# Moving the remaining key, query and value loads of a fused attention and MLP kernel into its MLP stages, with a fourth output buffer

## The chip, the cores and the metric

The kernel runs on one core of a Trainium2 chip. The metric is the device time of one execution in microseconds (us), taken as the median of several runs. The core's engines are named as the profile names them: PE (matrix multiply) and PEld (its weight loads, which overlap the multiplies), DVE (vector engine), ACT (activation engine), POOL (GpSimd) and SP (which here only issues DMAs). A DMA issued by POOL goes through queue 0 of the profile ("software_dynamic"), one issued by SP or ACT through queue 1 ("hardware_dynamic"). Each engine works through its own list of instructions in order and waits on semaphores for the others.

## The reference

Forgetting attention for 8 batches of 8 heads, 576 positions, head size 64, and then an MLP with a tanh-gelu over the 4608 rows that come out of it. Cut to what is computed:

```python
scores = scale * q @ k.T                     # per batch and head
log_f  = log(clip(f, 1e-4, 1.0)); cum = cumsum(log_f)
scores = where(causal, -1e9, scores + cum[:, None] - cum[None, :])
attn   = softmax(scores) @ v                 # [8, 8, 576, 64]
x      = attn.transpose(0, 2, 1, 3).reshape(4608, 512)
h      = x @ w_in                            # [4608, 2048]
out    = gelu_tanh(h) @ w_out                # [4608, 512] f32
```

All inputs are float32 in HBM; the weights and q, k are cast to bf16 on the way in, by the DMA.

## The kernel before

**Units of work.** Attention is done by quads: a quad is four heads of one batch, so there are 16 quads, two to a batch (quad 6 and 7 belong to batch 3, quad 8 and 9 to batch 4, and so on). The MLP is done by chunks of 512 rows, nine of them, 0 to 8. The rows of chunk c need the batches up to c, so the program runs the MLP of chunk c beside the attention of the quads 2c+2 to 2c+4.

**Stages.** For the chunks 1 to 7 the order alternates between two stages. In the MLP stage of chunk c the first matrix product and its gelu run (`P` and `R` in the tables, lines 363 and 412; PE writes `ps_h`, `ps_ab`, `ps_cd`). Its multiplies have 128 columns of weights each. In the attention stage that follows, the scores, the softmax and the value products of two quads (`S`, `D`, `V`; PE tiles `ps_s`, `po`) are woven between pieces of the second matrix product of the same chunk (`f`, line 497; PE tile `ps_w`), and there nearly every multiply is cut into four of 32 columns that run side by side, so this stage has many more PE instructions for each microsecond.

**What sets the order.** The order of all work is written out by hand, in tables of words that are played in order (`run`, line 709, for `FRONT`, which holds the start and chunks 0 and 1; `play`, line 747, for `TABLES[2]` to `TABLES[8]`). A word's place fixes where its instructions stand in the list of each engine that it uses. In the tables `q3` and `q4` stand for quads 2c+3 and 2c+4, `q5` and `q6` for 2c+5 and 2c+6; a word for a quad above 15 does nothing. The words that matter here:

- `LK.i` and `LQ.i` (line 190): POOL issues the load of quad i's keys or queries, 288 KB each, into `k_c[i % 2]` or `q_c[i % 2]`. There are two buffers of each, so a load has to wait until quad i-2 has been transposed out of its buffer.
- `TK.i` and `TQ.i` (lines 205 and 208): DVE transposes them into `kT` and `qT`.
- `LV.b.half` in `FRONT` and `LV` in the tables (lines 165, 665, 743): SP issues the five loads of the values of half a batch or of a whole one into `v_nat[b % 2]`; in `TABLES[c]` it is batch c+2. `LX.b.half` is the same issued by POOL. `@LK.6` after a word makes its first DMA wait for that load to land.
- `M.i.r` (line 271): POOL masks round r of a quad's scores with `affine_select`, after ACT's exponential (line 269). `VW.i` (line 211): POOL multiplies the values by the decay weights; `vw.i` does so on DVE.
- `S.i.r` (line 243): PE scores and ACT's exponential of round r of a quad. `CL.i`: a small DVE copy. `K` and `T`: DVE sums for the first product's blocks.
- `O.512`: what is left of the second product of the chunk before.

**Where the loads stand before.** In `TABLES[2]` all of `LK.q5 LQ.q5 LK.q6 LQ.q6 LV` lie in the MLP stage. In `TABLES[3]` and `TABLES[4]` the loads of `q5` lie in the MLP stage and those of `q6` (quad 12 and quad 14) in the attention stage, behind `M.q3.2`. In `TABLES[5]` `q6` would be quad 16, which does not exist. In `FRONT`, `LQ.8` lies inside the attention stage of chunk 1, and `LK.7`, `LK.8` and the five loads of `LX.3.1` (quad 7's values) lie at its end, on POOL.

**Buffers.** The results of the second product go through `o_st`, tiles of 128x512 float32 in a ring of three (`ostage_pool`, line 119), from which SP stores them. The gate input f is read into `f_sb` (line 149), used in the first microseconds only. `g1`, `g2`, `g4` (trace name `gsum`) hold sums of gelu outputs and are first written in the MLP stage of chunk 1.

Of the kernel before, what the change touches and what calls it, by code (L numbers as in the profile page):

```python
# [16 lines left out]
def kernel(  # L17
# [770 lines left out]
```

## Time and profile before

| | us |
|---|---|
| median of 3 runs | 330.29 (330.05 to 330.64) |
| the profiled execution | 330.31 |
| its span, from first to last instruction | 328.6 |
| PE busy in it | 315.0 |
| DVE busy | 231.8 |
| ACT busy | 202.2 |
| POOL busy | 111.6 |

The granted clock of PE was 0.999 of full speed over the span. The profile counts an engine as busy while one of its instructions runs; matrix multiplies overlap each other, so a busy PE need not be at its peak. Where an engine stood idle, the profile names what ended the wait. "issue" means that it found nothing that the engine waited for: no semaphore of another engine and no DMA of the program. Beside the queues of the program's own DMAs, the profile shows queues of kind "instruction": packets that bring code. Queue shares are shares of the time of 16 DMA engines.

### The profile page before, as it was taken

How to read it: one execution, taken by the hardware profiler on the slowest of the kernel's cores; microseconds unless marked ns; L12 is line 12 of the kernel's file. 1: busy time of each engine (PE TensorE's matmuls, PEld its weight loads, DVE VectorE, ACT ScalarE, POOL GpSimd, SP SyncE). 2: the span in 40 equal slices, each digit the busy share in tenths (PEclk: the TensorE clock that was granted, in tenths of full speed). 3: DMA queues.
4: the chain of work that ended last, by engine and by line, in shares of the span. 5: the costliest groups of instructions: out<-in, count | busy, mean ns of one | idle time of the engine just before them, and what ended most of it. 6: DMA issues, size and time to landing. Idle time of an engine off the chain costs nothing.

```text
span 328.6 us, 12085 instructions
## 1 busy us (share of the span) xinstructions
PE 315.0 (96%) x5443; PEld 211.7 (64%) x5463; DVE 231.8 (71%) x363; ACT 202.2 (62%) x239; POOL 111.6 (34%) x155
## 2 busy tenths in 40 slices
PE   3999999999999999999979999999999999999995
PEld 1357844545775467656756577657775787687684
DVE  4686139894876865778856997798778658785772
ACT  4685677775766676668637785678666841721630
POOL 8986563510415318102740248022720150000000
PEclk9999999999999999999999999999999999999999
DMA  7999999861125990284158615581020103012002
GB/s 127 206 210 215 164 229 205 161 159 38 36 40 106 240 213 9 68 177 74 36 108 182 100 38 104 146 128 50 33 69 2 34 6 98 0 34 96 3 33 96
DMA packets 44324, 33.43 MB, mean 102 GB/s; under 512 B 27488, under 2 KB 37856, under 8 KB 44272
## 3 DMA queue, kind: packets, MB, share of 16 engines
q0 software_dynamic: 8848, 16.58, 28.9%
q1 hardware_dynamic: 35280, 16.01, 18.9%
q8 instruction: 42, 0.69, 0.9%
q14 instruction: 10, 0.08, 0.1%
q10 hardware_dynamic: 144, 0.07, 0.1%
HBM read 36.85 MB, written 9.44 MB: 141 GB/s over the span
## 4 chain that ended last, share of the span: by engine, by line
PE 93%; POOL 2%; issue 2%; ACT 1%; DVE 1%; DMA 1%; POOLq 0%; DVEq 0%; ACTq 0%
PE ps_w L510 29%; PE ps_h L374 25%; PE ps_s L261 10%; PE po L329 10%; PE ps_h L464 4%; PE pso L580 4%; PE ps_cd L422 4%; PE ps_ab L422 3%; PE po_m L315 1%; PE idle_ps L240 1%; ACT pt L269 1%; POOL v_nat L169 1%; DMA out_dram<-o_st 1%; PE ps_o L329 0%; DVE pt L304 0%
## 5 line engine op out<-in xcount | busy, mean ns | idle before, releaser
L269 ACT ACTIVATE pt<-ps_s 128x1024 bf16<-128x1024 f32 (+2 forms) x100 | 93.7, 988 | 41.4 <-PE ps_s L261 36.9
L374 PE MATMUL ps_h<-xT,w_in_sb 128*128 128x512 bf16 x368 | 85.5, 379 | 0.8
L381 ACT ACTIVATE gT<-ps_h 128x1024 bf16<-128x1024 f32 x48 | 49.0, 1021 | 42.9 <-PE ps_h L374 42.8
L275 POOL TENSOR_SCALAR_AFFINE_SELECT pt<-pt 128x512 bf16<-128x512 bf16 (+3 forms) x65 | 39.1, 611 | 99.4 <-ACT pt L269 98.4
L374 PEld LDWEIGHTS <-w_in_sb 128*128 128x128 bf16 x384 | 37.4, 98 | 40.9 <-issue 0.4
L510 PEld LDWEIGHTS <-gT 128*32 128x32 bf16 (+1 forms) x1247 | 51.3, 97 | 6.3 <-issue 1.7
L510 PE MATMUL ps_w<-w_out_sb,gT 128*32 128x256 bf16 (+1 forms) x1050 | 47.2, 273 | 0.0
L510 PEld LDWEIGHTS <-gsum 128*32 128x32 bf16 (+1 forms) x1256 | 39.3, 97 | 3.2 <-issue 1.9
L261 PE MATMUL ps_s<-qT,kT 32*128 32x64 bf16 (+5 forms) x896 | 37.0, 265 | 0.5 <-issue 0.4
L198 DVE STREAM_TRANSPOSE kT<-k_c 128x576 f32<-128x576 f32 x16 | 20.0, 1248 | 17.6 <-DMA k_c<-in_k_dram 17.6
L510 PE MATMUL ps_w<-usum,gsum 128*32 128x256 bf16 (+1 forms) x832 | 30.8, 273 | 0.0
L535 DVE TENSOR_TENSOR o_st<-ps_w,snap 128x512 f32<-128x512 f32 x31 | 21.3, 690 | 13.0 <-PE ps_w L510 12.1
L215 POOL TENSOR_TENSOR vw<-v_nat,wT 128x1280 bf16<-128x1280 f32 (+1 forms) x13 | 30.4, 2337 | 0.1
L360 DVE TENSOR_TENSOR xT<-po,rb 128x576 bf16<-128x576 f32 x26 | 19.6, 754 | 12.8 <-PE po L329 12.5
L261 PEld LDWEIGHTS <-kT 32*128 32x128 bf16 x896 | 17.0, 93 | 17.6 <-issue 12.5
L192 POOL DMA_DIRECT2D k_c<-in_k_dram x16 | 9.2, 576 | 44.0 <-DVE kT L198 38.8
L329 PE MATMUL po<-pt,vw 128*32 128x64 bf16 (+4 forms) x624 | 22.9, 279 | 0.0
L329 PEld LDWEIGHTS <-vw 128*32 128x32 bf16 x672 | 14.5, 96 | 10.7 <-issue 4.0
L198 DVE STREAM_TRANSPOSE qT<-q_c 128x576 f32<-128x576 f32 x16 | 19.9, 1244 | 1.1 <-DMA q_c<-in_q_dram 1.1
L489 DVE TENSOR_TENSOR gsum<-gT 128x1024 bf16<-128x1024 bf16 x16 | 11.0, 685 | 11.0 <-ACT gT L381 11.0
L510 PE MATMUL ps_w<-w_out_sb,gsum 128*32 128x256 bf16 (+1 forms) x400 | 15.6, 273 | 1.7 <-issue 1.7
L169 POOL DMA_DIRECT2D v_nat<-in_v_dram x20 | 15.3, 775 | 4.6 <-DMA w_out_sb<-in_moe_w_out_dram 4.6
(100 smaller groups left out, 398.0 us busy)
## 6 DMA issues: line engine op xcount, KB each, us to landing
out_dram<-o_st SPq DMA_DIRECT2D x35, 256.0 KB, 2.2
k_c<-in_k_dram POOLq DMA_DIRECT2D x16, 288.0 KB, 4.9
q_c<-in_q_dram POOLq DMA_DIRECT2D x16, 288.0 KB, 5.5
v_nat<-in_v_dram SPq DMA_DIRECT2D x16, 256.0 KB, 4.7
w_in_sb<-in_moe_w_in_dram POOLq DMA_DIRECT2D x4, 512.0 KB, 9.3
w_out_sb<-in_moe_w_out_dram POOLq DMA_DIRECT2D x4, 512.0 KB, 8.4
v_nat<-in_v_dram SPq DMA_DIRECT2D x16, 128.0 KB, 3.0
v_nat<-in_v_dram POOLq DMA_DIRECT2D x13, 128.0 KB, 7.2
```

The source lines that it names most:

```text
L198: nc.vector.transpose(out=dst.rearrange("p s c -> p (s c)").bitcast(FP32) .rearrange("p (t a) -> p a t", a=S // 32), in_=src.rearrange("p ...
L215: eng.tensor_mul(vw[i % 2][:, t0:t1], vb[:, t0:t1, h0:h0 + 4, :], wT[:, i, t0:t1, :].unsqueeze(3).to_broadcast([128, t1 - t0, 4, D]))
L261: nc.tensor.matmul(tiles[h // 2][:, h % 2, c0:c0 + nq], key_columns(i, key, h, c), qq[32 * h:32 * h + 32, q0:q0 + nq, c], start=(c == 0 an ...
L269: nc.scalar.activation(p[:, 2 * g:2 * g + 2, off:off + n], t[:, :, 0:n], AF.Exp, scale=scale)
L275: nc.gpsimd.affine_select(out=x, in_=x, compare_op=ALU.is_ge, fill=0.0, base=0, pattern=pattern, channel_multiplier=-1)
L329: nc.tensor.matmul(po[r0:r0 + w.shape[-1], 448 + q0:448 + q0 + nq], w, p[:, h, col:col + nq], start=(key in (0, "low")), stop=(key in ("lo ...
L360: nc.vector.tensor_mul(xT[:, 2 * u + x, S * b + s0:S * b + s1], po, rbs[i, part])
L374: nc.tensor.matmul(ph[:, j, :], w_in_sb[:, dt, 128 * ft:128 * ft + 128], xT[:, dt, CH * c:CH * (c + 1)], start=(dt == 0), stop=(dt == N_DT ...
L381: nc.scalar.activation(gT[:, 2 * pr:2 * pr + 2, :], ph, AF.Gelu_apprx_tanh)
L422: nc.tensor.matmul(ps[:, j], w[:, dt, 128 * j:128 * j + 128], x[:, dt], start=(first and j == 0 and dt == 0), stop=(dt == 1), skip_group_c ...
L510: nc.tensor.matmul(ps[c0:c0 + width, n, cols[0]:cols[1]], x[:, j, 128 * n + c0:128 * n + c0 + width], w[:, j, cols[0]:cols[1]], start=(fir ...
L535: nc.vector.tensor_add(st, ps, kept[name])
```

## The change

The loads change places, on three edits of tables, and two buffers change.

1. `FRONT`: `LV.3.1` (SP) follows `LV.3.0@LQ.7`; `LK.7 LQ.8 LK.8` follow `M.4.0`; all in the MLP stage of chunk 1. `LQ.8` inside the attention stage and `LK.7 LK.8` and `LX.3.1@LK.6` at its end are gone. So the five value loads pass from POOL's queue to SP's.
2. `TABLES[3]` and `TABLES[4]` lose `LK.q6 LQ.q6` from the attention stage; `TABLES[4]` and `TABLES[5]` begin with `Y O.512 LK.q4 LQ.q4`, which are the same quads, 12 and 14, one chunk later. `TABLES[5]` also loses `LK.q6 LQ.q6`, which did nothing.
3. The ring of `o_st` has four tiles; `f_sb` is no tile of its own any more but the first 576 float32 of the first 64 partitions of `g2`.

No instruction of PE, DVE or ACT is added, removed or moved in its engine's order; POOL's list loses five DMA issues and SP's gains five.

```diff
@@ FRONT
-        v.3.0 f.0.3 H.4.2.0 CL.4 I.1.0 m.4.1 U.0 LV.2.1@LQ.5 I.1.4 TQ.6 m.4.2.3 I.1.1 I.1.5 U.1 LV.3.0@LQ.7 m.4.2.2 TK.6 G.0 M.4.0 I.1.2 I.1.3 U.3
-        I.1.6 I.1.7 G.1.1.2 U.2 X F.1.16 S.5.0 f.1.26 S.5.1 D.4 M.5.0 f.1.16 S.5.2 V.4.0 m.5.2.3 f.1.10 VW.5 V.4.1 CL.5 m.5.2.2 LQ.8 S.6.0 f.1.10 M.5.1
-        D.5 f.1.7 S.6.1 V.5.1 f.1.12 V.5.0 vw.6 S.6.2 m.6.1 M.6.2.2 m.6.0 m.6.2.3 LK.7 LK.8 CL.6 LX.3.1@LK.6
...
+        LQ.7 VW.4 H.4.0.0 V.3.1 v.3.0 f.0.3 H.4.2.0 CL.4 I.1.0 m.4.1 U.0 LV.2.1@LQ.5 I.1.4 TQ.6 m.4.2.3 I.1.1 I.1.5 U.1 LV.3.0@LQ.7 LV.3.1 m.4.2.2
+        TK.6 G.0 M.4.0 LK.7 LQ.8 LK.8 I.1.2 I.1.3 U.3 I.1.6 I.1.7 G.1.1.2 U.2 X F.1.16 S.5.0 f.1.26 S.5.1 D.4 M.5.0 f.1.16 S.5.2 V.4.0 m.5.2.3
+        f.1.10 VW.5 V.4.1 CL.5 m.5.2.2 S.6.0 f.1.10 M.5.1 D.5 f.1.7 S.6.1 V.5.1 f.1.12 V.5.0 vw.6 S.6.2 m.6.1 M.6.2.2 m.6.0 m.6.2.3 CL.6
@@ TABLES[3]
-        TK.q4 TQ.q4 M.q3.1 VW.q3 f.18 S.q3.2 V.q2.1 M.q3.2 LK.q6 LQ.q6 CL.q3 f.16 S.q4.0 VW.q4 D.q3 M.q4.0 f.18 S.q4.1 V.q3.0 M.q4.1 f.9 V.q3.1 f.7 T
+        TK.q4 TQ.q4 M.q3.1 VW.q3 f.18 S.q3.2 V.q2.1 M.q3.2 CL.q3 f.16 S.q4.0 VW.q4 D.q3 M.q4.0 f.18 S.q4.1 V.q3.0 M.q4.1 f.9 V.q3.1 f.7 T CL.q4
@@ TABLES[4]
-        Y O.512 P.0.1 R.1 P.4.1 R.1 R.1 TK.q3 TQ.q3 LK.q5 LQ.q5 M.q2.2 LV P.2 G.0 P.3 P.6 P.7 G.1.1.2 X F.10 S.q3.0 D.q2 M.q3.0 f.22 S.q3.1 V.q2.0
-        TK.q4 TQ.q4 M.q3.1 VW.q3 f.18 S.q3.2 V.q2.1 K.3.0 K.3.1 M.q3.2 LK.q6 LQ.q6 CL.q3 f.16 S.q4.0 VW.q4 D.q3 M.q4.0 f.18 S.q4.1 V.q3.0 K.3.2 M.q4.1
+        Y O.512 LK.q4 LQ.q4 P.0.1 R.1 P.4.1 R.1 R.1 TK.q3 TQ.q3 LK.q5 LQ.q5 M.q2.2 LV P.2 G.0 P.3 P.6 P.7 G.1.1.2 X F.10 S.q3.0 D.q2 M.q3.0 f.22
+        S.q3.1 V.q2.0 TK.q4 TQ.q4 M.q3.1 VW.q3 f.18 S.q3.2 V.q2.1 K.3.0 K.3.1 M.q3.2 CL.q3 f.16 S.q4.0 VW.q4 D.q3 M.q4.0 f.18 S.q4.1 V.q3.0 K.3.2
...
@@ TABLES[5]
-        Y O.512 P.0.1 R.1 P.4.1 R.1 R.1 TK.q3 TQ.q3 LK.q5 LQ.q5 M.q2.2 LV P.2 G.0 P.3 P.6 P.7 G.1.1.2 X F.10 S.q3.0 D.q2 M.q3.0 f.22 S.q3.1 V.q2.0
+        Y O.512 LK.q4 LQ.q4 P.0.1 R.1 P.4.1 R.1 R.1 TK.q3 TQ.q3 LK.q5 LQ.q5 M.q2.2 LV P.2 G.0 P.3 P.6 P.7 G.1.1.2 X F.10 S.q3.0 D.q2 M.q3.0 f.22
...
-    ostage_pool = ctx.enter_context(tc.tile_pool(name="ostage", bufs=3))
+    ostage_pool = ctx.enter_context(tc.tile_pool(name="ostage", bufs=4))
...
-    f_sb = singles.tile([BH, S], FP32, name="f_sb")
+    f_sb = g2.rearrange("p t n -> p (t n)").bitcast(FP32)[0:BH, 0:S]
```

More of the change, by code (lines that the diff above doesn't have):

```diff
@@ L74 @@
         TQ.0 B.2.256 TK.1 SB TR LP.2@LQ.0 B.2.128 CW S.0.0 B.5.384 B.1.256 Z TQ.1 vw.0.0 S.0.2 WI.0 LQ.2 M.0.0 B.3.384 H.1.0.1 LP.3 B.1.256 vw.1.0
-        WI.1@LU.4 W H.1.1.1 WI.3 B.2.256 WI.2 H.1.0.0 M.1.0.1 D.0.0 M.1.0.0 H.0.1.1 V.0.0.0 H.0.1.0 B.2.256 M.0.1 H.1.1.0 V.0.1.0 D.1.0 H.0.3.0 B.2.128
-        V.1.0.0 LX.1.1 H.0.3.1 V.1.1.0 m.0.3.2 H.1.3.0 m.0.3.4 B.1.256 VW.1.1 H.1.3.1 B.4.128 vw.0.1 D.0.1 M.1.3 S.1.2 M.1.1 LK.2 V.0.1.1 V.0.0.1 WO.0
-        J.0.1 D.1.1 J.0.0 WO.1@LV.1.1 V.1.1.1 V.1.0.1 J.0.3 WO.2@WI.1 VW.3 J.1.0 WO.3 LK.3 LQ.3 J.1.1 TQ.2 J.1.3 LQ.4 LX.1.0@WO.2 TK.2 J.0.2 J.1.2 X
@@ L82 @@
-        D.5 f.1.7 S.6.1 V.5.1 f.1.12 V.5.0 vw.6 S.6.2 m.6.1 M.6.2.2 m.6.0 m.6.2.3 LK.7 LK.8 CL.6 LX.3.1@LK.6
+        WI.1@LU.4 W H.1.1.1 WI.3 B.2.256 WI.2 H.1.0.0 M.1.0.1 D.0.0 M.1.0.0 H.0.1.1 V.0.0.0 H.0.1.0 B.2.256 M.0.1 H.1.1.0 V.0.1.0 D.1.0 H.0.3.0
+        B.2.128 V.1.0.0 LX.1.1 H.0.3.1 V.1.1.0 m.0.3.2 H.1.3.0 m.0.3.4 B.1.256 VW.1.1 H.1.3.1 B.4.128 vw.0.1 D.0.1 M.1.3 S.1.2 M.1.1 LK.2 V.0.1.1
+        V.0.0.1 WO.0 J.0.1 D.1.1 J.0.0 WO.1@LV.1.1 V.1.1.1 V.1.0.1 J.0.3 WO.2@WI.1 VW.3 J.1.0 WO.3 LK.3 LQ.3 J.1.1 TQ.2 J.1.3 LQ.4 LX.1.0@WO.2 TK.2
@@ new lines @@
+        J.0.2 J.1.2 X LK.4 F.0.6 TK.3 B.3.256 S.2.0 LK.5 F.0.9 S.2.2 F.0.10 S.2.1 TQ.3 TQ.4 F.0.10 LV.2.0@LK.5 m.2.1 vw.2 TK.4 S.3.0 f.0.1 M.2.2
+        CL.2 LQ.5 M.2.0 D.2 f.0.6 S.3.1 m.3.0 F.0.6 V.2.0 S.3.2 TK.5 LK.6 M.3.2 f.0.7 V.2.1 CL.3 S.4.1 m.3.1 LQ.6 F.0.6 TQ.5 H.4.2.1 D.3 H.4.0.1
+        LQ.7 VW.4 H.4.0.0 V.3.1 v.3.0 f.0.3 H.4.2.0 CL.4 I.1.0 m.4.1 U.0 LV.2.1@LQ.5 I.1.4 TQ.6 m.4.2.3 I.1.1 I.1.5 U.1 LV.3.0@LQ.7 LV.3.1 m.4.2.2
+        TK.6 G.0 M.4.0 LK.7 LQ.8 LK.8 I.1.2 I.1.3 U.3 I.1.6 I.1.7 G.1.1.2 U.2 X F.1.16 S.5.0 f.1.26 S.5.1 D.4 M.5.0 f.1.16 S.5.2 V.4.0 m.5.2.3
```

10 lines of the change are left out of this document (4 added, 6 removed).

## The prediction

> **What bounds the kernel now.** I read the page first: engines, then the DMA queues.
>
> ```profile
> span 328.6 us, 12085 instructions
> PE 315.0 (96%) x5443; PEld 211.7 (64%) x5463; DVE 231.8 (71%) x363; ACT 202.2 (62%) x239; POOL 111.6 (34%) x155
> ...
> q8 instruction: 42, 0.69, 0.9%
> ```
>
> PE is busy all but 13.6 us of the span, and none of the moved work is PE's, so a gain can only come from the places where PE waits. The third line is code: 42 packets of 0.69/42 MB, 16.4 KB. PE has 5443 + 5463 = 10,906 instructions, 260 for each of these packets. No other engine has a tenth as many, so queue 8 brings PE's program, a block of about 260 instructions at a time.
>
> Second, the windows view with one row per stage, from chunk 1's attention to chunk 6's MLP (columns: stretch; its length; busy time and instructions of PE, PEld, DVE, ACT, POOL; granted clock; DMA share; GB/s).
>
> ```profile
> 81.39:102.18 20.79, 20.74 (x614) 15.96 (x613) 16.25 (x25) 14.96 (x17) 5.26 (x5) 1.00 0.22 56
> 102.18:115.72 13.54, 13.49 (x63) 6.19 (x64) 8.98 (x12) 8.63 (x10) 7.57 (x12) 1.00 0.96 181
> 115.72:137.92 22.20, 21.70 (x641) 16.28 (x639) 14.99 (x27) 14.73 (x17) 9.44 (x10) 1.00 0.43 98
> 137.92:151.07 13.15, 13.10 (x75) 7.37 (x76) 10.49 (x13) 8.97 (x12) 2.36 (x4) 1.00 0.77 141
> 151.07:173.97 22.90, 21.14 (x639) 15.99 (x639) 16.67 (x29) 14.71 (x17) 10.35 (x12) 1.00 0.34 74
> 173.97:187.12 13.15, 13.09 (x75) 7.39 (x76) 10.44 (x13) 9.01 (x12) 2.36 (x4) 1.00 0.78 141
> 187.12:208.05 20.93, 20.88 (x640) 15.92 (x639) 17.54 (x29) 14.71 (x17) 10.62 (x12) 1.00 0.35 78
> 221.20:242.14 20.94, 20.89 (x640) 15.95 (x640) 16.01 (x26) 14.71 (x17) 9.22 (x10) 1.00 0.18 50
> 242.14:255.28 13.14, 13.09 (x75) 7.40 (x76) 9.81 (x14) 8.99 (x12) 1.23 (x2) 1.00 0.07 24
> ```
>
> The four attention stages of chunks 2 to 5 (rows 3, 5, 7, 8) hold the same PE work, yet take 22.20, 22.90, 20.93 and 20.94 us. So chunk 2 loses 1.27 us and chunk 3 loses 1.97 against chunk 4. The MLP stages lose nothing to transfers: 13.15 us with a DMA share of 0.77, 13.14 with 0.07. An attention stage runs about 1280 PE and PEld instructions in 21 us, an MLP stage 151 in 13 us: code is used up five times as fast in attention.
>
> Third, the timeline of PE inside the two long stages (start, busy, what, idle before it).
>
> ```profile
> 121.28 0.63 PE L261 MATMUL ps_s<-qT,kT 32*128 32x64 bf16 x15 [0.43 <-issue]
> 170.80 0.40 PE L510 MATMUL ps_w<-w_out_sb,gsum 128*32 128x256 bf16 x8 [1.71 <-issue]
> ```
>
> Both stops are "issue": no semaphore and no program DMA was waited for, and both fall in the middle of a run of like multiplies. Fourth, the code packets near them, in the DMA view of short windows (packets, MB, share of 16 engines' time): 162.3 to 168.5, 164.5 to 168.5 and 168.5 to 169.5 (one row each), then 117.1 to 118.9 and 118.9 to 119.9. The first, second and fourth have no row for queue 8.
>
> ```profile
> q0 software_dynamic: 285, 0.59, 60.0%
> ...
> q0 software_dynamic: 285, 0.59, 93.0%
> ...
> q8 instruction: 1, 0.02, 5.9%
> ...
> q0 software_dynamic: 159, 0.33, 95.3%
> ...
> q8 instruction: 1, 0.02, 5.8%
> ```
>
> No code packet starts in the 6.2 us up to 168.5, while queue 0 moves 0.59 MB, which is just `LK.12` and `LQ.12`. When that is through, the code packet comes at once (5.9% of 16 engines over 1.0 us: 0.94 us long), and PE goes on at 170.80, 1.3 us after it has landed. At 118.9 the same: queue 0 full before it, then a packet of 0.93 us, and PE on at 121.28, 1.4 us after landing. The windows view cut at code packets gives the rhythm (the first row in a stage without loads, the last at the start of chunk 1's attention).
>
> ```profile
> 231.11:234.83 3.72, 3.72 (x140) 2.91 (x136) 2.23 (x5) 2.48 (x4) 3.39 (x4) 1.00 0.02 4
> 162.25:168.54 6.29, 6.29 (x220) 4.53 (x212) 3.85 (x6) 3.88 (x4) 5.51 (x7) 1.00 0.66 116
> 165.07:169.09 4.02, 4.02 (x135) 2.81 (x124) 2.17 (x4) 2.04 (x3) 3.17 (x4) 1.00 0.96 200
> 117.08:120.85 3.77, 3.77 (x133) 2.94 (x126) 2.97 (x6) 3.48 (x5) 0.61 (x2) 1.00 1.13 220
> 84.12:88.52 4.40, 4.40 (x160) 3.59 (x156) 3.71 (x5) 3.33 (x5) 2.07 (x3) 1.00 0.19 63
> ```
>
> Undisturbed, one packet follows the other after 276 instructions and 3.72 us. In chunk 3 432 instructions went by between two. PE stands still when it has run one block (259 instructions, rows 3 and 4) since the next one was due. So a packet may be late by the block's time less 0.94 and less 1.3 to 1.4: in chunk 3, 4.02 - 2.24 = 1.8 us, in chunk 2, 3.77 - 2.33 = 1.4. It was due at 165.07 and came at 168.54, 3.5 late: 1.7 too much, and PE stood 1.71. In chunk 2 it was due at 117.08 and came at 118.9, 1.8 late: 0.4 too much, and PE stood 0.43. The rest of the loss (1.97 - 1.71 = 0.26 and 1.27 - 0.43 = 0.84) follows in shorter stops, since the packets behind a late one come late too. This is my theory: POOL's key and query loads hold back PE's code, and only the attention stage is quick enough to feel it.
>
> **The change, part by part.** *Quad 12 (`TABLES[3]` to `[4]`).* POOL's rows now:
>
> ```profile
> 163.25 0.59 POOL L192 DMA_DIRECT2D k_c<-in_k_dram  x1
> 163.84 0.54 POOL L192 DMA_DIRECT2D q_c<-in_q_dram  x1
> 168.62 0.64 POOL L275 TENSOR_SCALAR_AFFINE_SELECT pt<-pt 128x512 bf16<-128x512 bf16 x1 [0.79 <-ACT pt L269]
> 204.67 0.64 POOL L275 TENSOR_SCALAR_AFFINE_SELECT pt<-pt 128x512 bf16<-128x512 bf16 x1 [0.51 <-ACT pt L269]
> ```
>
> POOL takes nothing of `O.512` or `Y`, so the two issues follow chunk 3's last mask, at 168.62 + 0.64 = 169.26, not in the MLP stage proper. The first packet came 1.25 us or more after the issue at 163.25 (the windows from 162.3 and from 164.5 hold the same 285), so queue 0 fills from about 170.5. The code due at 165.07 then meets no load. The next is due one block later, 169.1, and is through (0.94) before 170.5; were it late by another 3.5 us it would cost nothing, for the block behind it is used in the MLP stage, where 151 instructions last 13.15 us. Gain: 1.97 us, at least the 1.71 of the single stop. VW and the mask behind the old place start 1.1 us earlier, and nobody waits for POOL there. `TK.12` stands in the attention stage of chunk 4, some 20 us after the load.
>
> *Quad 14.* The same move in chunk 4, where the loads cost nothing (20.93 against 20.94 without). They go behind the mask that ends at 205.31, with packets from 206.5, and the code after that feeds chunk 5's MLP stage: 0. Bounds: no gain is left there; if a packet of the end of chunk 4 were hit as in chunk 3, +1.97.
>
> *Quads 7, 8 and batch 3.* The sizes, from the page (KB each, median us to landing), and chunk 2's start:
>
> ```profile
> k_c<-in_k_dram POOLq DMA_DIRECT2D x16, 288.0 KB, 4.9
> ...
> v_nat<-in_v_dram POOLq DMA_DIRECT2D x13, 128.0 KB, 7.2
> ...
> 102.93 1.08 POOL L192 DMA_DIRECT2D k_c<-in_k_dram  x2
> 104.00 3.66 POOL L169 DMA_DIRECT2D v_nat<-in_v_dram  x5
> 112.23 0.53 POOL L192 DMA_DIRECT2D q_c<-in_q_dram  x1 [0.55 <-DVE qT L198]
> ...
> 107.44 1.25 DVE L198 STREAM_TRANSPOSE kT<-k_c 128x576 f32<-128x576 f32 x1 [3.21 <-DMA k_c<-in_k_dram]
> ...
> 104.72 11.10 SPq L169 DMA_DIRECT2D v_nat<-in_v_dram  x5
> ```
>
> `TK.7` waits 3.21 us for `LK.7`, and `LK.9` to `LQ.10`, each issued when a transpose has freed its buffer, end at 112.23 and queue behind what is left of 1.15 MB (two loads of 288 KB, and values of 576 KB: four of 128 and a half one). That is why queue 0 is still full at 118.9. With these transfers gone to chunk 1, `TK.7` starts 3.21 us earlier and the last issue is at 109.0. Queue 0 moved 0.33 MB in 1.8 us beside the values (the row of 117.1 to 118.9), 0.18 MB/us, so 1.15 MB from about 107 take 6.4 us, to 113.5, over 3 us ahead of the code due at 117.08. The values on queue 1 are 1.15 MB more; at the stage's 0.181 MB/us for all queues together (its row) 2.3 MB from 105 would last until 117.7, at the 0.220 of the 117.08 row until 115.5. So the end is near, but queue 0 is clear. Gain: the 1.27 us of chunk 2. Bounds: 0, if code is still late, and 1.27.
>
> In chunk 1's MLP stage the five value loads come behind the ten that SP issues there, and three key and query loads join them.
>
> ```profile
> 68.10 6.02 SPq L169 DMA_DIRECT2D v_nat<-in_v_dram  x10
> ...
> 86.32 1.48 POOL L275 TENSOR_SCALAR_AFFINE_SELECT pt<-pt 64x256 bf16<-64x256 bf16 x2 [18.90 <-ACT pt L269]
> ```
>
> `LK.8` waits for `TK.6`, which on DVE stands ahead of the first sum into `gsum` (75.58, below); behind it on POOL stands a mask that idles 18.90 us anyway. On SP nothing else is due before that stage's first store. In all 15 x 128 KB at most and 3 x 288 KB, 2.7 MB; at 0.22 from 69 to 81.3, about the stage's end. Its PE loses only 20.79 - 20.74 = 0.05 us in the attention stage: 0, at most 0.05 gained by taking `LQ.8` out.
>
> *Ring of four, and f in `g2`.* The waits of `o_st`'s writer, the first use of `gsum` and the last of `f_sb`:
>
> ```profile
> L535 DVE TENSOR_TENSOR o_st<-ps_w,snap 128x512 f32<-128x512 f32 x31 | 21.3, 690 | 13.0 <-PE ps_w L510 12.1
> ...
> 75.58 0.69 DVE L489 TENSOR_TENSOR gsum<-gT 128x1024 bf16<-128x1024 bf16 x1 [2.07 <-ACT gT L381]
> ...
> L613 PE MATMUL ps_lt<-ident_f,f_sb x5: 311/311/336, 5.0 to 5.4; 64*128 64x64 f32 x4, 64*64 64x64 f32 x1
> ```
>
> DVE's adds into `o_st` waited for PE, 12.1 of 13.0 us; no DMA is named, so a fourth tile frees nobody. `gsum` is first written at 75.58, f last read at 5.4. Both 0; if stores were late by the whole remaining 0.9 us, that would be the most to gain.
>
> The Trainium skill, "Runtime: NRT & Kernel Launch", section "Instruction fetch mechanics", has code come in 16 KiB blocks of 256 instructions, which the q8 row bears out, and gives PE room for 2048 instructions; by that a packet 3.5 us late would starve nobody and the sum would be 330.3. The trace disagrees: a stop after 259 instructions.
>
> The sum against the profiled execution: 330.31 - 1.97 - 1.27 = 327.07, its span 328.6 - 3.24 = 325.4. The median stands 0.02 lower: 327.05.
>
> **The rivals.** (a) *Only chunk 3 gains*: queue 1's values, ending between 115.5 and 117.7, keep the code late in chunk 2. For: that range spans 117.08. Against: late packets go with a full queue 0. 330.31 - 1.97 = 328.3. (b) *Only chunk 2 gains*, because in chunk 3 the stores of `o_st` now meet the code: 329.0. Against: chunk 5 has these stores and no loss. (c) *No change*: code comes late for a reason of its own, at that place of the program, and the loads only happen to be there: 330.3. For: the profile names no releaser. Against: chunk 5, with the same PE work and no such loads, has no stop, and twice the code came just when queue 0 had emptied. The Trainium skill, "DMA: Bandwidth & Descriptors", section "Queues, rings and completion order", has a DMA engine take turns between queues packet by packet; by that code would wait for one load packet only, and the time would be (c)'s 330.3. The trace disagrees: 285 load packets went by without a turn for code. (d) *Slower*: loads overrun the MLP stages of chunks 1 and 2. It decides where 2.7 MB take longer than 69 to 85.8, 1.8 us past the first code packet of chunk 1's attention (84.1): below 0.16 MB/us. Two code packets there would come late as in chunk 3, +3.94, and chunk 2 would keep its 1.27: 330.31 + 3.94 - 1.97 = 332.3. For: queue 0 alone moved 0.59 MB in 4.0 us (the row from 164.5), 0.15. Against: with both queues at work 0.18 to 0.22.
>
> **How the numbers follow.** Both gains 0.70, (a) 0.12, (b) 0.05, (c) 0.06, (d) 0.07. A measurement of this kernel tells 0.2%, 0.66 us, from no change. The first three are faster by more: 0.87; (c) is the same, 0.06; (d) slower, 0.07. The time is that of both gains. The range goes from 326.3 (0.7 for runs and for small stops that I did not count) to 328.8, which takes in (a).
>
> **What would show it.** Right: no idle by "issue" over 0.3 us in the attention stages of chunks 2 and 3, both near 20.9 us, code packets 3.7 us apart in them; `TK.7` without a wait; POOL's loads of quads 12 and 14 right behind the last mask; MLP stages unchanged at 13.15. Wrong: a stop that has moved into chunk 1 or chunk 4, a code packet late with queue 0 empty, or a stage of chunk 3 still near 22.9 with its loads gone.

## The result, and the profile after

| | before | after |
|---|---|---|
| median of the runs side by side, us | 330.36 (330.05 to 330.64) | 326.59 (326.07 to 326.78) |
| ratio | | 0.9884, 95% interval 0.9866 to 0.9901 |
| profiled execution, us | 330.31 | 326.78 |
| its span, us | 328.6 | 325.1 |

The changed kernel takes 1.2% less. From the page of the changed kernel, the lines that stood first in the prediction:

```profile
span 325.1 us, 12081 instructions
...
PE 314.0 (97%) x5443; PEld 211.5 (65%) x5463; DVE 232.4 (71%) x363; ACT 202.1 (62%) x239; POOL 107.7 (33%) x150
...
q8 instruction: 42, 0.69, 1.0%
```

PE has the same instructions and the same 42 code packets, POOL five fewer. The span fell by 3.5 us, PE's busy time by only 1.0: the rest is time in which PE stood. The windows view, one row per stage from chunk 1's MLP to chunk 5's MLP, without chunk 3's MLP (columns as in the prediction):

```profile
67.86:81.47 13.61, 13.55 (x63) 6.21 (x64) 9.62 (x13) 9.15 (x9) 1.23 (x3) 1.00 1.07 206
81.47:102.26 20.79, 20.74 (x614) 15.98 (x612) 16.24 (x25) 14.95 (x17) 4.66 (x4) 1.00 0.16 47
102.26:115.80 13.54, 13.49 (x63) 6.20 (x64) 9.06 (x12) 8.62 (x10) 2.90 (x5) 1.00 0.84 164
115.80:136.73 20.93, 20.88 (x640) 15.95 (x639) 15.64 (x27) 14.72 (x17) 9.51 (x10) 1.00 0.22 59
...
149.88:170.81 20.93, 20.88 (x639) 15.95 (x639) 16.00 (x26) 14.71 (x17) 10.29 (x12) 1.00 0.20 43
170.81:183.96 13.15, 13.09 (x75) 7.36 (x76) 10.74 (x14) 9.00 (x12) 2.29 (x4) 1.00 0.95 195
183.96:204.90 20.94, 20.89 (x641) 15.95 (x640) 17.51 (x29) 14.72 (x17) 10.56 (x12) 1.00 0.20 46
204.90:218.04 13.14, 13.09 (x75) 7.38 (x76) 10.74 (x14) 8.98 (x12) 2.29 (x4) 1.00 0.91 192
```

Chunk 2's attention is at 20.93 (22.20 before), chunk 3's at 20.93 (22.90). No other stage has changed: chunk 1's attention 20.79 as before, and the MLP stages that took up the loads, with DMA shares of 1.07, 0.95 and 0.91, are not longer. Chunk 1's MLP stage before, which neither the prediction nor the table above shows:

```profile
67.78:81.39 13.61, 13.55 (x63) 6.22 (x64) 9.51 (x13) 9.15 (x9) 0.00 (x0) 1.00 0.44 106
```

The same view of the kernel after, cut at the first code packets of chunk 2 and at those of chunk 3:

```profile
117.14:120.87 3.73, 3.73 (x140) 3.01 (x136) 2.97 (x5) 3.50 (x5) 0.55 (x2) 1.00 0.11 23
...
152.94:157.32 4.38, 4.38 (x160) 3.61 (x156) 3.75 (x7) 3.56 (x5) 1.07 (x2) 1.00 0.17 55
157.32:160.73 3.41, 3.41 (x128) 2.70 (x120) 3.22 (x5) 2.61 (x4) 2.94 (x2) 1.00 0.06 16
160.73:164.46 3.73, 3.73 (x144) 2.88 (x132) 2.36 (x5) 2.02 (x3) 3.58 (x4) 1.00 0.04 9
164.46:168.20 3.74, 3.74 (x136) 2.77 (x128) 1.91 (x4) 1.94 (x2) 1.75 (x4) 1.00 0.23 74
```

The packets come every 3.4 to 4.4 us and PE never stands (its busy time equals the length of each window). The instructions that moved, in the timelines of DVE and POOL:

```profile
104.22 1.25 DVE L198 STREAM_TRANSPOSE kT<-k_c 128x576 f32<-128x576 f32 x1
...
109.00 0.53 POOL L192 DMA_DIRECT2D q_c<-in_q_dram  x1 [0.55 <-DVE qT L198]
...
168.02 0.59 POOL L192 DMA_DIRECT2D k_c<-in_k_dram  x1
169.51 0.55 POOL L192 DMA_DIRECT2D q_c<-in_q_dram  x1 [0.90 <-DVE o_st L535]
```

`TK.7` waits for nothing and starts at 104.22; the last load of chunk 2's MLP stage is issued at 109.00; quad 12's loads follow chunk 3's last mask.

What the stages do not show is the rest of the gain. They give 1.27 + 1.97 = 3.24 us, the span fell by 3.5. The last row of SP, before and then after:

```profile
325.11 0.42 SPq L550 DMA_DIRECT2D out_dram<-o_st  x1
```

```profile
321.94 0.42 SPq L550 DMA_DIRECT2D out_dram<-o_st  x1
```

That store's issue moved by 3.17 us, and from it to the end it is 3.48 us before and 3.14 after (spans of 328.58 and 325.08 less these starts). The trace's semaphore records of SP at the end of the program show why (start, event, the semaphore that is waited for; those of the last stores are marked):

```
before                                after
325.57 wait S106                      322.40 wait S106
327.11 wait S108   a last store       322.47 wait S108
327.31 wait S112   the last store     322.54 wait S112
327.37 wait S113                      322.60 wait S113
327.44 wait S114                      322.66 wait S114
327.49 wait S115                      323.66 wait S115   a last store
327.56 wait S116                      323.95 wait S116   a last store
327.62 wait S117                      324.12 wait S117   the last store
327.68 wait S118                      324.18 wait S118
327.74 drain                          324.24 drain
```

SP asks for each of its DMA semaphores in turn, 0.06 us each where the DMA has landed. Before, the last store's is the third in the list, and the waits behind it are paid after it has landed (327.31 to 327.74, 0.43 us). The change gives SP five more loads, the eight semaphores that the stores and loads use in turn shift by five, the last store now uses the eighth in the list, and the waits ahead of it pass while it is still on its way (324.12 to 324.24, 0.12 us). The runs of the next section bear this out: e1, which leaves SP's list alone, has the end of before (3.47 us, the last store's semaphore third), e2 and e12, which give SP the five loads, that of after (3.12 and 3.13 us, eighth).

### The profile page after: what moved, and what is told of

It reads as the page before. It is cut to its first block, busy times and chain, and to the rows that moved or that the text cites. A ratio compares the mean times of both kernels' runs of the same rounds, so it can differ in the third digit from the quotient of the medians.

```text
span 325.1 us, 12081 instructions
## 1 busy us (share of the span) xinstructions
PE 314.0 (97%) x5443; PEld 211.5 (65%) x5463; DVE 232.4 (71%) x363; ACT 202.1 (62%) x239; POOL 107.7 (33%) x150
## 4 chain that ended last, share of the span: by engine, by line
PE 94%; POOL 2%; issue 1%; ACT 1%; DVE 1%; POOLq 0%; DVEq 0%; ACTq 0%
PE ps_w L510 30%; PE ps_h L374 25%; PE ps_s L261 10%; PE po L329 9%; PE ps_h L464 4%; PE pso L580 4%; PE ps_cd L422 4%; PE ps_ab L422 3%; PE po_m L315 1%; PE idle_ps L240 1%; ACT pt L269 1%; POOL v_nat L169 1%; PE ps_o L329 0%; DVE pt L304 0%; POOL q_c L192 0%
## 5 line engine op out<-in xcount | busy, mean ns | idle before, releaser
L535 DVE TENSOR_TENSOR o_st<-ps_w,snap 128x512 f32<-128x512 f32 x31 | 21.3, 689 | 11.0 <-PE ps_w L510 10.0
L510 PE MATMUL ps_w<-usum,gT 128*128 128x256 bf16 (+1 forms) x197 | 16.4, 273 | 0.0
L493 DVE TENSOR_TENSOR gT<-gT 128x1024 bf16<-128x1024 bf16 x16 | 15.3, 958 | 0.2
```

What stands on the lines that cost most here:

```text
L510: nc.tensor.matmul(ps[c0:c0 + width, n, cols[0]:cols[1]], x[:, j, 128 * n + c0:128 * n + c0 + width], w[:, j, cols[0]:cols[1]], start=(fir ...
L535: nc.vector.tensor_add(st, ps, kept[name])
```

## The experiments

Twelve kernels. In the table, "due" is the start of the PE instruction in the trace's records behind which an undisturbed code packet comes (number 189 + 256 k of PE and PEld together, in order of start: the last of a block; in the attention stages, packets with no load in their way come mostly within 1 us of it, at most 1.3 after it; the traces of before and after lack 20 of PE's records, which moves "due" there by some 0.2 us), "late" is the packet's start less that, and "lost" is the length of the stage less that of the same stage undisturbed (20.79 in chunk 1, 20.93 in the others). "At block starts" is what was lost on the first instruction of a block, number 190 + 256 k; it is explained below the table.

| kernel | stage | due | came | late | lost | at block starts | median of the runs |
|---|---|---|---|---|---|---|---|
| before | chunk 2 | 117.08 | 118.92 | 1.8 | 1.27 | 0.6 + 0.4 + 0.3 | 330.36 |
| before | chunk 3 | 165.07 | 168.54 | 3.5 | 1.97 | 2.0 | |
| e1 | chunk 2 | 116.40 | 118.34 | 1.9 | 0.56 | 0.55 | 327.52 (327.07 to 328.08) |
| e2 | chunk 3 | 163.53 | 165.21 | 1.7 | 0.68 | 0.69 | 327.14 (326.45 to 328.64) |
| e3 | chunk 1 | 91.43 | 93.22 | 1.8 | 0.42 | 0.41 | 329.85 (327.52 to 331.65) |
| e3 | chunk 2 | 117.18 | 119.18 | 2.0 | 0.99 | 0.61 + 0.39 | |
| e3 | chunk 3 | 164.98 | 168.36 | 3.4 | 1.96 | 1.96 | |
| e4 | chunk 3 | 164.00 | 165.75 | 1.75 | 0.39 | 0.39 | 327.23 (326.92 to 328.79) |
| e5 | chunk 5 | 231.30 | 232.74 | 1.4 | 0.01 | 0 | 327.56 (326.54 to 328.37) |
| e6 | chunk 5 | 230.94 | 233.46 | 2.5 | 0.79 | 0.79 | 327.11 (326.53 to 328.06) |
| e7 | chunk 5 | 231.08 | 234.01 | 2.9 | 1.24 | 1.24 | 326.91 (326.46 to 327.93) |
| e10 | chunk 5 | 231.32 | 233.17 | 1.85 | 0.77 | 0.30 | 327.36 (326.96 to 329.77) |

One execution of a kernel differs from the next by more than some of the losses, so what is lost is read from the stage in the profiled execution, not from the medians. The medians of the kernel before that ran beside these lay between 330.37 and 330.6.

For "at block starts" the records of PE and PEld in a stage were lined up, instruction by instruction, with those of the same stage in a kernel that lost nothing there (e12 for the chunks 1 to 3, e11 for chunk 5). Except in e10, the whole loss falls on one to three instructions, each the first of a block, and each started 1.1 to 1.5 us after its block's packet had landed. In no stage from chunk 1 on does any of e1 to e12 start a block sooner than 1.1 us after its packet has landed. So PE stops where its code ends. The idle time by "issue" understates these stops (0.43 us in chunk 2 of before, 1.71 in chunk 3, none in e4): the ends of multiplies are modelled, and those of the multiplies ahead reach into the stop.

**e1, the tables alone** (`FRONT` and the buffers as before):

```diff
@@ TABLES[3], TABLES[4]
-  ... M.q3.2 LK.q6 LQ.q6 CL.q3 ...
+  ... M.q3.2 CL.q3 ...
@@ TABLES[4], TABLES[5]
-  Y O.512 P.0.1 ...
+  Y O.512 LK.q4 LQ.q4 P.0.1 ...
```

> The kernel before with the moves of quads 12 and 14 alone (tables 3 to 5); start table, ring and f as before. Theory A (the loads of POOL's queue hold back PE's code): chunk 3's attention stage falls from 22.90 to 20.9 us, chunk 2's stays at 22.2 with its stop at 121.28; 330.36 - 1.97 = 328.4 us. Rival B (the gain comes from work that waits for the loaded data or stands behind the issues on POOL): nothing waits for quad 12's data in chunk 3, so the stage stays near 22.9 and the time near 330.4.

Ratio to before 0.9892 (0.9837 to 0.9947). Chunk 2's and chunk 3's attention in the windows view, and PE's stop in its timeline:

```profile
115.23:136.72 21.49, 21.14 (x642) 16.04 (x639) 14.96 (x27) 14.72 (x17) 9.36 (x10) 1.00 0.45 102
...
149.86:170.79 20.93, 20.93 (x641) 15.93 (x639) 16.27 (x27) 14.70 (x17) 10.28 (x12) 1.00 0.23 48
```

```profile
120.72 0.64 PE L261 MATMUL ps_s<-qT,kT 32*128 32x64 bf16 x15 [0.35 <-issue]
```

Chunk 3 is free of its loss, chunk 2 stops at the same multiply as before, but lost 0.56 in this execution, not 1.27, and the median is 0.9 us below the 328.4 that were expected.

**e2, the front alone** (`LV.3.1` to SP, `LK.7 LQ.8 LK.8` behind `M.4.0`; tables and buffers as before):

```diff
@@ FRONT
-  ... LV.3.0@LQ.7 m.4.2.2 TK.6 G.0 M.4.0 I.1.2 ... m.5.2.2 LQ.8 S.6.0 ... LK.7 LK.8 CL.6 LX.3.1@LK.6
+  ... LV.3.0@LQ.7 LV.3.1 m.4.2.2 TK.6 G.0 M.4.0 LK.7 LQ.8 LK.8 I.1.2 ... m.5.2.2 S.6.0 ... CL.6
```

> The kernel before with the move of the loads of quads 7, 8 and batch 3 alone (the start table). Theory A: chunk 2's attention stage falls from 22.20 to 20.9 us, chunk 3's keeps its stop of 1.7 us and 22.9 us; 330.36 - 1.27 = 329.1 us. Rival B: the 3.21 us that the transpose of quad 7's keys waited are what counts; they lie under the MLP stage (13.54 us, PE full), so the time stays near 330.4.

Ratio 0.9887 (0.9818 to 0.9957). Chunk 2 is clean. The rest of the expectation, 22.9 us for chunk 3 and 329.1 in all, was missed: chunk 3, whose loads are where they were before, lost only 0.68 (windows view). POOL's timeline and the DMA view of 163.1 to 165.2 and 165.2 to 166.2 show what differs:

```profile
149.64:171.25 21.61, 21.20 (x642) 16.00 (x639) 16.66 (x29) 14.71 (x17) 10.33 (x12) 1.00 0.36 78
```

```profile
161.82 0.59 POOL L192 DMA_DIRECT2D k_c<-in_k_dram  x1
162.68 0.55 POOL L192 DMA_DIRECT2D q_c<-in_q_dram  x1 [0.27 <-issue]
```

```profile
q0 software_dynamic: 147, 0.31, 100.9%
...
q0 software_dynamic: 62, 0.13, 81.0%
q8 instruction: 1, 0.02, 10.9%
```

Before, `LQ.12` was issued without a gap behind `LK.12` (163.25 and 163.84, the rows in the prediction), and the code came behind both, 285 packets later. Here POOL paused 0.27 us between the two, and the code came between the two loads, behind 147 packets. The trace's records of POOL show what stands in the pause: three waits for semaphores of earlier DMAs, which in before and e3 are all ahead of `LK.12` (163.03, 163.11 and 163.20 in before), begin in e2 and e4 between the two issues (162.66 in e2), under other semaphore numbers. `FRONT` is the only edit of e2, so its moves put the waits there; that the pause is what let the code in is argued from these four runs, not shown alone. Chunk 3 lost 1.97 and 1.96 with the old front, 0.68 and 0.39 (e4, below) with the new one. So 1.97 is no fixed price of these loads, and the gains of the two moves do not add up: each alone gives most of what both give.

**e3, the buffers alone:**

```diff
-    ostage_pool = ctx.enter_context(tc.tile_pool(name="ostage", bufs=3))
+    ostage_pool = ctx.enter_context(tc.tile_pool(name="ostage", bufs=4))
...
-    f_sb = singles.tile([BH, S], FP32, name="f_sb")
+    f_sb = g2.rearrange("p t n -> p (t n)").bitcast(FP32)[0:BH, 0:S]
```

> The kernel before with the ring of four and f inside g2 alone. As predicted: no effect, 330.36 us, both stages as before. Second theory, from the ends of the two traces: before, the last pieces of the output waited for a store (the chain of waits ends with a store of 1.91 us at 322.56), in the changed kernel they did not, and its last stretch from the last ps_l of the first half (321.20 before, 318.03 after) to the end is 0.35 us shorter; so 330.36 - 0.35 = 330.0 us, all of it in the last 5 us.

Ratio 0.9989 (0.9955 to 1.0023), no difference that the interval can tell. Its span is that of before, 328.6, and the end is that of before too (the last store is issued at 325.11 in both), so the second theory fell. Chunk 3 lost 1.96, as before. Chunk 1's attention lost 0.42 in this execution:

```profile
81.26:102.47 21.21, 20.99 (x613) 16.05 (x612) 16.23 (x25) 14.94 (x17) 5.26 (x5) 1.00 0.22 55
...
151.09:173.98 22.89, 21.20 (x641) 15.99 (x639) 16.40 (x28) 14.71 (x17) 10.33 (x12) 1.00 0.32 71
```

There `LQ.8` was the load that held the code back, as it did not in the profiled execution of before. So taking it out of chunk 1's attention is worth something in some executions.

**e4, the kernel after, with quad 12's loads back in chunk 3's attention** (`TABLES[3]` and the start of `TABLES[4]` as before):

> The changed kernel with the two loads of quad 12 put back behind the mask in chunk 3's attention stage. Theory A: the code packet that is due about 0.6 us after the burst begins comes some 3.5 us late, PE stands 1.5 to 2 us in chunk 3, its stage is 22.5 to 23.0 us again and the time 326.6 + 1.97 = 328.6 us. The exact size hangs on where the code packet falls in the burst. Rival B: 326.6 us.

Ratio 0.9892 (0.9834 to 0.995). Expected were 1.5 to 2 us of stop and 328.6 us. Chunk 3 lost 0.39:

```profile
150.11:171.43 21.32, 21.20 (x641) 16.01 (x639) 16.35 (x28) 14.71 (x17) 10.33 (x12) 1.00 0.36 77
```

As in e2 POOL paused 0.28 us between the two loads, and the code came behind the first one. With the loads the loss is there, without them (after, e1) it is not; its size goes with the order in which the transfers and the code come.

**e5 to e8, transfers added where nothing was lost.** To the kernel after, loads into buffers that nobody reads any more are added in chunk 5's attention, which has no loads of its own and took 20.93 us:

```diff
@@ TABLES[5]
-  ... M.q3.2 CL.q3 ...
+  ... M.q3.2 EK EQ CL.q3 ...      e5: keys and queries, 288 KB each, by POOL
+  ... M.q3.2 EK CL.q3 ...         e6: keys alone
+  ... M.q3.2 EV CL.q3 ...         e7: the five loads of one batch's values, 1.15 MB, by SP; e8: by POOL
```

> The changed kernel, and in chunk 5's attention stage, which has no loads, two loads more on POOL (288 KB each, keys and queries of quad 0 into buffers that nothing reads any more), at the place where chunk 3 had its two. Nobody waits for their data. Theory A (code is served in order of arrival behind what POOL has already queued): the code packet due at 231.6 comes late, behind one load (about 1.7 us late, no stop or one up to 0.5 us) if it is asked for before the second load is queued, behind both (3.5 us late, stop of 1.7 us) if after; chunk 5's stage 21.0 to 22.9 us instead of 20.93, the time 326.7 to 328.6 us. Rival B (loads cost only through what waits for their data or stands behind them on POOL): 20.93 us, 326.6 us.

> The same with one load more in place of two (288 KB, keys of quad 0). Theory A: the code packet is at most one load, 1.9 us, late; that is about the slack of 1.4 to 1.8 us, so a stop of 0 to 0.4 us, chunk 5's stage 20.9 to 21.3 us, and never more than with two. Rival B: 20.93 us.

> The changed kernel, and in chunk 5's attention stage five loads of values more (1.15 MB, batch 0 into a buffer that nothing reads any more), issued by SP, in the same 4 us as the loads of the runs with extra loads. Theory A (it is POOL's queue that holds code back): code packets at most 0.5 us late, no stop, 20.9 to 21.0 us. Rival C (any transfer of that size holds code back): 1.15 MB take 5 us, twice the two loads of quad 12; code at least 3 us late, stop over 1 us, stage over 22 us.

> The same five loads of values, same bytes and same packets, issued by POOL behind the mask of that stage. Theory A, in order of arrival: the code packet due at 231.6 waits for the load or two that are queued by then (1.5 to 3.5 us late), the next one for the rest; chunk 5's stage 21.2 to 22.9 us. Theory A2 (POOL's queue goes before code as long as it has anything): code waits for all five loads, 6 us and more late, a stop of 4 us or more, stage over 24 us. Rival B: 20.93 us.

Ratios 0.992 (0.9889 to 0.9952), 0.9908 (0.9877 to 0.9939), 0.9904 (0.9873 to 0.9935) and 0.9898 (0.9867 to 0.9929). Chunk 5's attention in the windows views of e5, e6, e7 and e8:

```profile
217.95:238.89 20.94, 20.94 (x641) 15.97 (x639) 16.00 (x26) 14.70 (x17) 10.32 (x12) 1.00 0.34 78
```

```profile
217.59:239.31 21.72, 21.12 (x642) 15.90 (x640) 15.99 (x26) 14.71 (x17) 9.78 (x11) 1.00 0.26 61
```

```profile
217.73:239.90 22.17, 21.12 (x641) 15.89 (x639) 16.00 (x26) 14.71 (x17) 9.20 (x10) 1.00 0.40 99
```

```profile
217.80:238.73 20.93, 20.93 (x640) 15.89 (x639) 16.02 (x25) 14.71 (x17) 13.80 (x15) 1.00 0.40 105
```

Theory A missed all four, e5 by little (it had 21.0 us or more for e5, 21.3 at most for e6, no stop for e7 and 21.2 or more for e8); for e7 its rival C held. Two loads cost nothing and one cost 0.79, against the expectation that one never costs more than two. With two, the code came after 64 load packets, 1.4 us late; with one, it came behind 143 of the 144 (the DMA view of 231 to 233.4, which has no row for queue 8). SP's values cost 1.24, POOL's nothing. In e7 the values were moving from 229.5 on, and the code that was due at 231.08 came at 234.01, in the midst of them (e6's row first, then e7's DMA view of 231 to 234, with no row for queue 8, and of 234 to 235):

```profile
q0 software_dynamic: 143, 0.29, 87.4%
```

```profile
q1 hardware_dynamic: 2256, 0.57, 85.9%
...
q1 hardware_dynamic: 778, 0.20, 86.4%
q8 instruction: 1, 0.02, 6.0%
```

```profile
236.26 0.63 PE L329 MATMUL po<-pt,vw 128*32 128x64 bf16 x17 [1.05 <-issue]
```

The packet had landed at 234.98, and PE went on 1.3 us later, as in the prediction (the "1.05" is what the modelled ends leave of a stop of 1.24). So queue 1 holds the code back as queue 0 does, and "POOL's key and query loads" was too narrow. In e8 the code came at 231.43, just ahead of the burst's first packet at 231.66, and on time. The next code was 2.3 us late, behind 137 packets of POOL's values, and cost nothing, since it was used in the MLP stage (its first instruction started 8.6 us after it had landed). The two runs differ in more than the queue: the same values moved in packets of 0.25 KB on queue 1 (2256 in 0.57 MB) and of about 3 KB on queue 0 (311 in 1.01 MB), not in the same packets as was expected.

**e9 and e10, the same transfers one mask earlier**, so that the burst is moving when the code is due:

```diff
@@ TABLES[5]
-  ... V.q2.1 M.q3.2 CL.q3 ...
+  ... V.q2.1 EV M.q3.2 CL.q3 ...      e9: values by POOL
+  ... V.q2.1 EK EQ M.q3.2 CL.q3 ...   e10: keys and queries by POOL
```

> The kernel after, with the same five value loads (1.15 MB into buffers nobody reads any more) issued by POOL in chunk 5's attention, but one mask earlier than in e8, so that the burst is under way when a code packet is due near 231.1 us. First theory (what decides is whether a transfer of any queue is under way when the code is asked for, not which engine issued it): the packet due near 231.1 comes 2 to 3 us late, PE stands still once for 0.5 to 1.2 us, and chunk 5's attention takes 21.5 to 22.2 us instead of 20.93; the kernel is 0.6 to 1.3 us slower than after. Second theory (values issued by POOL are harmless, as e8 could also be read; only SP's queue or key and query loads hold code back): no stop over 0.3 us, 20.93 us, 326.6.

> The kernel after, with the two unread loads of 288 KB that e5 had, issued one mask earlier, so that the first of them is already moving when the code is due near 231.1 us. First theory (code waits for the transfers that were queued ahead of its own request; two loads of 288 KB take about 4 us on queue 0): the packet comes 2.4 us late or more, PE stands still 0.6 us or more, chunk 5's attention takes 21.6 us or more. Second theory (two loads get in each other's way and leave room for code between them, as in e5): 1.5 us late or less, no stop over 0.3 us, 20.93 us.

e9 took 332.69 us (331.72 to 333.6), ratio 1.0073 (1.0051 to 1.0096): slower than before, and for a reason that neither theory had. POOL's, then PE's timeline, then the windows view behind the stop:

```profile
228.62 4.30 POOL L169 DMA_DIRECT2D v_nat<-in_v_dram  x5 [0.30 <-POOL vw L215]
232.90 1.26 POOL L275 TENSOR_SCALAR_AFFINE_SELECT pt<-pt 128x512 bf16<-128x512 bf16 x2
```

```profile
233.63 0.31 PE L329 MATMUL po<-pt,w_bf 128*1 128x320 bf16 x4 [3.36 <-POOL pt L275]
```

```profile
234.22:238.00 3.78, 3.78 (x80) 2.82 (x79) 2.52 (x4) 0.00 (x0) 3.27 (x3) 0.55 0.43 86
```

Five issues of values keep POOL for 4.3 us, the mask stands behind them, and PE waits 3.36 us for it. After that stop PE was granted a clock of 0.55 on the mean of this window (1.00 in all the other stages shown; the trace's clock record has 0.5 from 234.63 to 238.04) and did 80 multiplies in 3.78 us where it does 140 otherwise. The stage took 26.53 us, 5.6 more. The case that e9 was made for did not arise: with PE stopped, no code was due near 231.1. One packet was due while the burst still moved, at 235.32; it came at 236.08, 0.8 us late, behind 33 packets of the burst, and cost nothing. So a burst does not always hold code back. e9 shows the price of POOL's issues ahead of a mask, which e8, with the same issues behind it, does not pay.

e10: ratio 0.9907 (0.9877 to 0.9938), the stage in the windows view, the DMA view of 229.4 to 233.1 and PE's timeline:

```profile
217.51:239.21 21.70, 21.31 (x642) 15.88 (x639) 15.99 (x26) 14.71 (x17) 10.29 (x12) 1.00 0.33 75
```

```profile
q0 software_dynamic: 282, 0.59, 93.3%
```

```profile
230.55 0.28 PE L329 MATMUL po<-pt,w_bf 128*1 128x192 bf16 x8 [0.28 <-POOL pt L275]
```

The code came when both loads were through, 1.85 us late, and the stage lost 0.77. The stage has the first theory's size, but by another sum: lined up with e11, 0.47 us are lost at PE's wait for the mask that the two issues pushed back (230.55), and 0.30 at the first instruction of the block whose code was late (235.57, 1.4 us after the packet had landed). A lateness of 1.85 us and a stop of 0.30 lie between the two theories, so e10 decides for neither.

**e11, the two unread loads behind chunk 5's last mask**, the place to which the change moves quads 12 and 14 in their chunks:

> The kernel after, with the same two unread loads behind chunk 5's last mask, the place to which the change moves quads 12 and 14. Theory: the code that is due while they move is used in the MLP stage, where 151 instructions last 13.15 us, so that even 3 us late costs nothing: no stop over 0.3 us, chunk 5's attention 20.93, its MLP stage 13.15, 326.6 us. Rival (the place behind the last mask is harmless in chunks 3 and 4 only by luck): a stop in the attention stage's end or at the MLP stage's start, 0.4 to 2 us, as for loads in mid-stage.

326.56 us (326.46 to 326.74), ratio 0.9888 (0.9847 to 0.9929). Chunk 5's attention and MLP stage:

```profile
217.87:238.80 20.93, 20.93 (x641) 15.90 (x640) 16.00 (x26) 14.71 (x17) 10.28 (x12) 1.00 0.19 43
238.80:251.94 13.14, 13.14 (x77) 7.38 (x76) 9.82 (x14) 8.99 (x12) 1.22 (x2) 1.00 0.31 73
```

The place is harmless here, but chunk 5 did not put it to the test: the loads moved from 237.3 to 241.9, the last code ahead of them had come at 235.31, 0.2 us late, and the next came at 244.85, long before it was used. Chunk 4 of the same run does: the code due at 204.3 came 1.7 us late, with quad 14's loads moving, and no stage is longer.

**e12, both moves without the buffers** (e1 and e2 together):

> The kernel before with both moves of loads and nothing else: the ring of three and f's own buffer stay. Theory (ring and f are worth nothing, the moves are the whole gain, and the end of the kernel follows from the five more value loads on SP): 326.6 us as after, span 325.1, every attention stage without a stop, the last store's issue to the end 3.1 us. Second theory (the fourth tile lets the last stores leave sooner or the stages run cleaner): 0.3 us or more slower than after, with adds that wait for a store or a tail of 3.4 us.

326.68 us (326.55 to 327.12), ratio 0.9887 (0.9839 to 0.9934), 0.09 from after. Chunks 2 and 3, and SP's last row:

```profile
116.16:137.09 20.93, 20.93 (x641) 15.93 (x639) 15.64 (x27) 14.72 (x17) 9.52 (x10) 1.00 0.22 60
...
150.24:171.17 20.93, 20.93 (x640) 15.93 (x639) 16.25 (x27) 14.70 (x17) 10.30 (x12) 1.00 0.22 46
```

```profile
322.30 0.42 SPq L550 DMA_DIRECT2D out_dram<-o_st  x1
```

From that row to the end of its span of 325.4 it is 3.1 us: the shorter end comes with the front's moves and not with the ring. The ring and f's place are worth nothing, alone (e3) and beside the moves (e12).

## Why the prediction was right, and where it was not

*The cause* held. Every packet of the table that was 1.7 us late or more cost its stage something, the one that was 1.4 us late nothing; the predicted slack was 1.4 to 1.8, and lateness less the first stop gives 1.2 to 1.7 (1.0 in e2, whose packet took 1.75 us in place of 0.94 to 1.0). Every stop for code stands at the start of a block, 1.1 to 1.5 us after the packet has landed, also in e4 and e10, where the profile's idle time shows none by "issue". Loads put into a clean stage make the stop, on queue 0 (e6) and on queue 1 (e7); code that is late but used up slowly does not (1.7 us in chunk 4 of e11, 2.3 us in e8, and 1.85 us at the end of chunk 4 in e2 and e3, where a block lasted 5.1 us and no time was lost).

*Quad 12, 1.97 us:* right in the profiled execution (22.90 to 20.93), but the size is not the price of the loads. With the same loads at the same place chunk 3 lost 0.68 in e2 and 0.39 in e4, where the new front had put POOL's waits between the two. Nor are the two gains independent, as the sum takes them: the moves of the tables alone took 327.52 us and those of the front alone 327.14, against 328.4 and 329.1 by the sum's terms.

*Quads 7, 8 and batch 3, 1.27 us:* right in size, by a step that was wrong. The prediction had queue 0 clear at 113.5, three us ahead of the code. The DMA view of after, from 105 to 117.1 and from 117.1 to 121, has it otherwise:

```profile
q0 software_dynamic: 576, 1.18, 56.2%
...
q1 hardware_dynamic: 380, 0.09, 11.0%
q8 instruction: 2, 0.03, 3.8%
```

Queue 0 began at 108.17, not at 107, and its last packet ended at 117.05; the code came at 117.14. 1.18 MB in 8.9 us are 0.13 MB/us, not the 0.18 that the sum took from a window in which queue 1 sent little. Even queue 1 went on past 117.1, which was rival (a)'s condition. That rival did not come about, because what was left was soon through: in the eleven kernels that have the edit of `FRONT` (after, e2, e4 to e12) this packet was up to 1.25 us late, within the slack of 1.4, and chunk 2 lost nothing. In the worst of them the gain was safe by tenths of a microsecond, not by three: that it came whole is in part luck.

*The shorter stops* that were to make up 1.27 - 0.43 = 0.84 in chunk 2 did come, but are not 0.84. The first stop is 0.6, not 0.43, and the starts of the next two blocks lost 0.4 and 0.3 more, each 1.3 to 1.5 us after its packet had landed. In chunk 3 there were none: the one stop is the whole 1.97, and the 0.26 that the prediction gave to shorter ones is what the modelled ends of multiplies hide of it. For the same reason the stage's busy time fell from 21.70 to 20.88 us for the same multiplies.

*Ring and f: 0; quad 14: 0; chunk 1: 0* in the profiled executions. For quad 14 the reason is the place of the block's end, not that no code was late: before, the packet due at 203.03 came 1.5 us late with its loads moving, and in e2 and e3 the same one 1.85 us, but the block that PE works through meanwhile lasts nearly to the end of the stage, 5.1 us in e2 and e3 in place of 3.7. For chunk 1 e3 shows that the 0.05 bound was too low: `LQ.8` there can cost 0.42.

*Rivals (b), (c) and (d):* fell. Chunk 3's attention is clean with the stores of `o_st` in it (20.93). The stop goes with the loads and comes back with them. The 2.9 MB (2.7 in the prediction, whose own terms of 15 x 128 KB and 3 x 288 KB are 2.85; 0.86 on queue 0, 2.03 on queue 1) of chunk 1's MLP stage were through at 82.58, 3.2 us ahead of the point from which (d) decided. One argument against (c) is weaker than it reads: the 285 load packets that passed "without a turn for code" were spread over 16 engines, about 18 on each (an estimate, 285/16), and the code packet used one (0.94 us of one engine are the 5.9% of 16 that the row shows). That does not show that no turns are taken, only that a turn, if there is one, is longer than one packet of the profile. What refutes (c) is that the loads were taken out and put back.

*The sum* was 327.07 for a profiled execution that took 326.78. The 0.3 us that it lacks are the end of the program (3.5 us from the last store's issue before, 3.1 after): five DMAs that pass to SP's queue shift the order in which its semaphores stand in the last waits. The prediction counted those DMAs in their stage and not in the list of the end.

## What to carry to other kernels

Where the profile puts a stop of PE down to "issue" in a stretch of many small multiplies, look at the instruction queue's packets: bulk transfers on either queue can hold the program's own code back, so put them where PE uses few instructions per microsecond, and measure the slack as the time of one block less the packet's time less the time from its landing to PE's next multiply. Ask of each issue that is moved on POOL what stands behind it: behind a mask five of them cost nothing, ahead of it 5.6 us. The idle time in the profile shows only a part of such a stop: line the starts of PE's instructions up with those of a clean stage, and look at every 256th. The size of such a loss in one profile is one outcome of several, so take its cause from the profile and its size from more than one run.

## What the runs showed of the hardware that was not expected

- A code packet can wait through a burst on queue 1 and then come in its midst (e7, 2.9 us late, with 778 packets of values in the microsecond in which it came), and one load of 288 KB can hold it longer (e6, 2.5 us) than two (e5, 1.4 us). What decides its turn is not settled: behind the first load (e2, e4, e6), behind both (before, e3, e10) and within the first (e5) were all seen, and in e9 a packet came 0.8 us after it was due in the midst of a burst.
- A late packet is made up slowly. In before the four packets behind chunk 2's late one started 3.5, 2.9, 2.6 and 2.5 us after the one ahead of each had landed, and 3.5 us is the least distance between two of them, against a use of one in 3.7: they were still 2.1, 1.6, 1.1 and 0.9 us late.
- After a stop of 3.4 us PE's granted clock was 0.5 for 3.4 us, from 1.0 us after its restart on (e9); behind the stop of 2.0 us in chunk 3 of before it was 1.00 (170.80 to 173.00).
- The order in which a queue's semaphores happen to be used is worth 0.3 us at the end of the program.
